# Two-stage attention and gated feed-forward kernel on one core: normalisation first in a step, an earlier first load, the decays of all heads later

## The chip, the cores and the metric

The kernel runs on one core of a Trainium2 chip. The metric is the device time of one execution in microseconds (us), lower being better. Differences of less than about 0.2% are not told from no change here.

## The reference

```python
# attention, B, H, S, D = 8, 8, 576, 64
scores = scale * np.matmul(q, k.transpose(0, 1, 3, 2))
log_f = np.log(np.clip(f, 0.0001, 1.0))
cum = np.cumsum(log_f, axis=-1)
decay = cum[:, :, :, None] - cum[:, :, None, :]
scores = np.where(causal, -1000000000.0, scores + decay)
scores = scores - np.max(scores, axis=-1, keepdims=True)
attn = np.exp(scores)
attn = attn / (np.sum(attn, axis=-1, keepdims=True) + 1e-09)
x = np.matmul(attn, v)                 # transposed and reshaped to 4608 x 512
# feed-forward, w_in 512 x 2048, w_out 2048 x 512
h = x @ w_in
sp = np.maximum(h, 0.0) + np.log1p(np.exp(-np.abs(h)))
out = (h * erf(sp)) @ w_out
```

`f` holds one gate for each head and position. Its clipped logarithm, summed along the sequence, is the decay that is added to the scores.

## The kernel before

The kernel has two stages. The first is the attention, which writes its output transposed to `xt_d` in HBM. The second is the feed-forward part (class `Moe`), which reads `xt_d` in chunks of 256 tokens. On TensorE (PE), VectorE (DVE), ScalarE (ACT) and GpSimd (POOL) the instructions stand in the order in which the code states them (`manual_schedule` with `ORDERED`, L20 and L230), and each engine works through its own list in that order. Only the DMA queue of SyncE (SP) is ordered by the scheduler.

**The step.** Heads are taken in 32 pairs, and each pair in two halves of its query blocks, so there are 64 units `t`, even and odd ones with other blocks (`BLOCKS`, `PARTS`, L34 to L42). The loop at L476 is a software pipeline. In step `t` it works on six units at once:

- `scores(t)` (L349): PE multiplies queries and keys of unit `t` into two PSUM tiles `s`, one for each head of the pair (`ps_s`, two buffers), and adds the causal mask (L363).
- `reduce(t, j)` (L373): DVE adds the decay `c` to the scores of head `j`, writes them to `pr` and takes the row extreme into `st`. With that the PSUM tile `s` of head `j` is free for `scores(t + 1)`.
- `exps(t - 1, j)` (L387): ACT applies Exp to `pr` in place and sums the rows into `st`.
- `normalize(t - 2)` (L394): DVE adds 1e-9 to the sums (L396) and takes reciprocals (L397). POOL then multiplies each row block of `pr` by its reciprocal (L401): four instructions for an even unit, six for an odd one.
- `transposes(t - 3, a)` (L404): PE transposes 128 x 128 blocks of `pr` into PSUM banks `t` (`ps_t`, three buffers): 12 blocks in three banks for an even unit, 13 in four for an odd one. `evacuate` copies a bank to `pt`: banks 0 and 1 by ACT (L422), banks 2 and 3 by DVE (L420, L418). Bank 3 takes the buffer of bank 0 again.
- `values(t - 4)` (L426): PE multiplies `pt` and the values into `o` (one PSUM buffer). `store(t - 5)` (L443): DVE copies `o` to `xo` (L449, L452, L453), and SP sends it to `xt_d`.

In an even step the transposes are thus those of an odd unit, and the other way round. One piece of weight conversion (`convert`, L277) stands near the end of each step from the fourth on: in turn ACT (L285), DVE (L289), DVE (L294 and L296), DVE with POOL (L299, L302, L303).

Before, DVE's list in a step reads: `store(t - 5)`, `reduce(t, 0)`, `reduce(t, 1)`, its evacuations of unit `t - 3`, `normalize(t - 2)`, `convert`.

**The start.** The pair 0 decays come from two rows of `f` that are broadcast to all partitions (`fd`): clip (L320, DVE), Ln (L321, ACT), running sum (L325, DVE), times -8 (L326, DVE). The same chain over all heads (`fr` to `cum`) goes to `cum_d` in HBM, and `load(p)` for later pairs broadcasts rows of `cum_d` into `c` (L340). Before, all of this stands ahead of the first step.

**The end of the attention.** For `t` from 64 to 67 each step also runs one `moe.step()` (L201): `up(j)` (PE, 24 matmuls, L126), `softplus(j)` (ACT, L132), and later `erf` and the gate. Softplus and Erf need other tables on ACT than Exp, so a table load stands before the first of them. Before, `moe.step()` stands last in the step. `load_x` and `split_x` (L100, L106) bring in a chunk of `xt_d` and split it in two parts on ACT (L111) and POOL (L112).

Of the kernel before, what the change touches and what calls it, by code (L numbers as in the profile page):

```python
# [11 lines left out]
F32 = mybir.dt.float32  # L12
# [9 lines left out]
P = 128  # L22
B, H, S, D = 8, 8, 576, 64
# [202 lines left out]
def attention_moe(ctx, tc, q2, k2, vp, f, w_in, w_out, out):  # L226
    nc = tc.nc
# [17 lines left out]
    cum_d = dram.tile([B * H, S], F32, name="cum_d")  # L245
# [10 lines left out]
    def wide4(nm):  # L256
        return cv.tile([P, 1024], F32, name=nm, tag="wide")

    moe = Moe(tc, xt_d, out, xp, wide4)
# [6 lines left out]
    def load_weight(u):  # L266

        a, i = divmod(u, 4)
        if i < 2:
            src = w_in[2 * i * P:2 * (i + 1) * P, a * 512:(a + 1) * 512].rearrange("(k p) n -> p k n", p=P)  # L270
        else:
            r = (2 * a + i - 2) * P
            src = w_out[r:r + P].rearrange("p (k n) -> p k n", k=2)
        raws[u] = raw = wide4(f"wraw{u}").bitcast(I32)
        nc.sync.dma_start(out=raw.rearrange("p (a n) -> p a n", a=2), in_=src)
# [35 lines left out]
    with ExitStack() as ph:  # L311
        early = ExitStack()
        wk = ph.enter_context(tc.tile_pool(name="wk", bufs=2))
# [5 lines left out]
        def log_clipped(x):  # L319
            nc.vector.tensor_scalar(out=x, in0=x, scalar1=1e-4, scalar2=1.0, op0=ALU.max, op1=ALU.min)  # L320
            nc.scalar.activation(out=x, in_=x, func=AF.Ln)  # L321

        def decay(out, x):

            nc.vector.tensor_tensor_scan(out=out, data0=x, data1=x, initial=0.0, op0=ALU.add, op1=ALU.bypass)  # L325
            nc.vector.tensor_scalar(out=out, in0=out, scalar1=-8.0, scalar2=None, op0=ALU.mult)  # L326
# [3 lines left out]
        def load(p):  # L330

            q = io.tile([P, PAD + S], F32, name=f"q{p}", tag="q")
            k = io.tile([P, S], F32, name=f"k{p}", tag="k")
            nc.sync.dma_start(out=q, in_=q2[p // NP, p % NP])
            nc.sync.dma_start(out=k, in_=k2[p // NP, p % NP])
            c = io.tile([P, 2, S], F32, name=f"c{p}", tag="c")
            if p:
                for j in range(2):
                    n = 2 * p + j
                    nc.sync.dma_start(out=c[:, j], in_=cum_d[n:n + 1].rearrange("a s -> (a s)").partition_broadcast(P))  # L340
            pairs[p] = [q, k, c]

        def load_values(p):

            v = wk.tile([P, 9, P], F32, name=f"v{p}", tag="v")
            nc.sync.dma_start(out=v, in_=vp[p // NP, p % NP].rearrange("p (c d) -> p c d", c=9))
            vals[p] = v
# [21 lines left out]
        def row(t, i, j):  # L369

            return probs[t][:, TOFF[i] + j * END[i]:TOFF[i] + (j + 1) * END[i]]

        def reduce(t, j):  # L373
            p, half = divmod(t, 2)
            c, s, st = pairs[p][2], raw_scores[t][j], stats[t]
            for m, i in enumerate(BLOCKS[half]):
                to, score, decay_ = (x.rearrange("p (k n) -> p k n", n=64) for x in (
                    row(t, i, j), s[:, SCOL[i]:SCOL[i] + END[i]], c[:, j, :END[i]]))
                nc.vector.tensor_tensor_reduce(  # L379
                    out=to[:, ::-1] if j else to, in0=score, in1=decay_, scale=-0.125, scalar=BIG,  # L380
                    op0=ALU.add, op1=ALU.min, accum_out=st[:, 0, j, m:m + 1])
            if j:
                del raw_scores[t]
                if half:
                    del pairs[p]

        def exps(t, j):  # L387
            st = stats[t]
            for m, i in enumerate(BLOCKS[t % 2]):
                seg = row(t, i, j)  # L390
                nc.scalar.activation(out=seg, in_=seg, func=AF.Exp, bias=st[:, 0, j, m:m + 1], scale=-1.0,  # L391
                                     accum_out=st[:, 1, j, m:m + 1])

        def normalize(t):  # L394
            st = stats.pop(t)
            nc.vector.tensor_scalar(out=st[:, 1], in0=st[:, 1], scalar1=1e-9, scalar2=None, op0=ALU.add)  # L396
            nc.vector.reciprocal(out=st[:, 2], in_=st[:, 1])  # L397
            for m, i in enumerate(BLOCKS[t % 2]):
                for j in range(2):
                    seg = row(t, i, j)  # L400
                    nc.gpsimd.tensor_scalar(out=seg, in0=seg, scalar1=st[:, 2, j, m:m + 1], scalar2=1.0,  # L401
                                            op0=ALU.mult, op1=ALU.mult)
# [12 lines left out]
        def evacuate(t, a):  # L415
            b, pt = banks.pop((t, a)), pts[t]
            if a == 3:
                nc.vector.tensor_copy(out=pt[:, 1536:], in_=b[:, 64:128])  # L418
            elif a == 2:
                nc.vector.tensor_copy(out=pt[:, 1024:1536], in_=b)  # L420
            else:
                nc.scalar.copy(out=pt[:, 512 * a:512 * a + 512], in_=b)  # L422
            if a == len(BANKS[t % 2]) - 1:
                del probs[t]
# [18 lines left out]
        def store(t):  # L443
            p, half = divmod(t, 2)
            o = held.pop(t)
            if half == 0:
                held["x"] = xo = wk.tile([P, S], F32, name=f"xo{p}", tag="xo")
                blocks = xo[:, 64:].rearrange("p (a q) -> p a q", a=4)
                nc.vector.tensor_copy(out=blocks[:, ::3], in_=o[:, :256].rearrange("p (a q) -> p a q", a=2))  # L449
            else:  # L450
                xo = held.pop("x")
                nc.vector.tensor_copy(out=xo[:, 192:448], in_=o[:, :256])  # L452
                nc.vector.tensor_copy(out=xo[:, :64], in_=o[:, 256:320])  # L453
                b, pp = divmod(p, NP)
                nc.sync.dma_start(out=xt_d[pp * P:(pp + 1) * P, b * S:(b + 1) * S], in_=xo)
                del vals[p]

        NH = B * H

        fd = [wk.tile([P, S], F32, name=f"fd{j}", tag=f"pt{j}") for j in range(2)]  # L460
        for j in range(2):
            nc.sync.dma_start(out=fd[j], in_=f[0, j].partition_broadcast(P))
        fr = wk.tile([B * H, S], F32, name="fr", tag="xo")
        nc.sync.dma_start(out=fr, in_=f.rearrange("b h s -> (b h) s"))
        load(0)
        for j in range(2):
            log_clipped(fd[j])
            decay(pairs[0][2][:, j], fd[j])
        log_clipped(fr)
        cum = wk.tile([B * H, S], F32, name="cum", tag="xo")  # L470
        decay(cum, fr)
        nc.sync.dma_start(out=cum_d, in_=cum)
        load(1)
        todo = pieces[1]
        load_weight(0)
        for t in range(NH + 5):  # L476
            there = [0 <= t - n < NH for n in range(6)]
            p, half = divmod(t, 2)
            if half == 0 and t + 4 < NH:
                load(p + 2)  # L480
            if half == 0 and there[2]:
                load_values(p - 1)
            if there[5]:
                store(t - 5)
            if there[0]:
                scores(t)
            if there[1]:
                exps(t - 1, 0)
            if there[0]:
                reduce(t, 0)  # L490
            if there[3]:
                for a in range(3):
                    transposes(t - 3, a)
                evacuate(t - 3, 0)
            if there[3] and len(BANKS[(t - 3) % 2]) == 4:
                transposes(t - 3, 3)
            if there[4]:
                values(t - 4)
            if there[1]:
                exps(t - 1, 1)  # L500
            if there[0]:
                reduce(t, 1)
            if there[3]:
                for a in range(1, len(BANKS[(t - 3) % 2])):
                    evacuate(t - 3, a)
            if there[2]:
                normalize(t - 2)
            if t >= 4 and todo:
                convert(*todo.pop(0))
            if t == NH - 2:  # L510
                moe.load_x(0)
                moe.split_x(0)
            if t == NH - 1:
                early.close()
                moe.ep = moe_pools.enter_context(tc.tile_pool(name="ep", bufs=2, side="right"))
                moe.ps_ha = moe_pools.enter_context(tc.tile_pool(name="ps_ha", bufs=4, space=PSUM, side="right"))
            if NH <= t < NH + 4:
                moe.step()
        assert not todo and not pts and not held and not vals

    w2 = ctx.enter_context(tc.tile_pool(name="w2", bufs=1))
# [44 lines left out]
```

## Time and profile before

| What | us |
|---|---|
| median of 3 runs | 1184.77 (1184.61 to 1186.2) |
| the profiled execution's own time | 1185.39 |
| its span in the profile | 1183.6 |
| PE busy | 1152.4 (97%) |
| DVE busy | 563.4 (48%) |
| ACT busy | 598.9 (51%) |
| POOL busy | 474.1 (40%) |

The own time of the profiled execution is 1.8 us more than the span from the first to the last instruction. PEld is the loading of PE's weights, which overlaps its matmuls. In a timeline row stand start, busy time, engine, line, operation, tiles, shape, count, and in brackets the idle time before the row with what ended it. A row can hold several instructions that follow each other. In a table of windows the engines' busy times in each stretch are followed by PEclk, the granted TensorE clock as a share of full speed. The attention fills the span to about 348 us, the feed-forward part the rest.

### The profile page before, as it was taken

Reading aid. Unit: us, or ns where it says so; the run is one execution under the profiler, and the core shown is the slowest. Engines: PE = TensorE matmul, PEld = TensorE weight load, DVE = VectorE, ACT = ScalarE, POOL = GpSimd, SP = SyncE. Lnnn points to the kernel's source line nnn. Section 1 sums busy time; section 2 is a strip of 40 time slices with the busy share of each in tenths; the row PEclk is TensorE's granted clock in tenths of the full one; section 3 lists DMA queues with packets and bytes.
Section 4 is the critical chain, followed back from the end, with each engine's and each line's share of the span. In section 5 each row is a group of like instructions: output and inputs, shape, how many; then the busy total and the mean of one; then the engine's idle time right before and its main releaser. Section 6 shows DMA issues by size and latency. Waiting matters only on the chain.

```text
span 1183.6 us, 22838 instructions
## 1 busy us (share of the span) xinstructions
PE 1152.4 (97%) x8992; PEld 1010.0 (85%) x8992; DVE 563.4 (48%) x1473; ACT 598.9 (51%) x1231; POOL 474.1 (40%) x531
## 2 busy tenths in 40 slices
PE   5999999999999999999999999999999999999998
PEld 3777777777779999999999999998999999998987
DVE  4888888888874665665322322321231231231221
ACT  3777777777775676565423422432432342242432
POOL 1565666555673444444432432232232232232221
PEclk9999999999999999999999999999999999999999
DMA  7566767667641222421221221210110110100000
GB/s 249 187 229 230 240 215 244 213 220 239 208 145 56 79 100 75 139 73 54 89 72 54 77 85 54 71 37 1 37 36 1 36 35 2 37 15 23 18 19 18
DMA packets 56618, 118.68 MB, mean 100 GB/s; under 512 B 4672, under 2 KB 19008, under 8 KB 56512
## 3 DMA queue, kind: packets, MB, share of 16 engines
q1 hardware_dynamic: 56512, 117.23, 30.2%
q8 instruction: 71, 1.16, 0.4%
q14 instruction: 35, 0.29, 0.1%
HBM read 93.47 MB, written 23.74 MB: 99 GB/s over the span
## 4 chain that ended last, share of the span: by engine, by line
PE 82%; DVE 9%; POOL 7%; issue 1%; ACT 1%; DMA 0%; POOLq 0%; ACTq 0%
PE ph L126 35%; PE y L165 11%; PE y L163 11%; PE y L164 11%; POOL pr L401 7%; DVE pr L379 6%; PE s L358 5%; PE o L440 4%; PE t L413 3%; DVE pt L420 2%; PE s L363 1%; DVE st L397 1%; DMA fd<-in_f_dram 0%; DVE c L325 0%; DVE st L396 0%
## 5 line engine op out<-in xcount | busy, mean ns | idle before, releaser
L126 PE MATMUL ph<-xh,w 128*128 128x256 f32 x2304 | 435.8, 282 | 0.0
L126 PEld LDWEIGHTS ph<-xh,w 128*128 128x128 f32 x2304 | 367.0, 191 | 5.9
L144 POOL TENSOR_TENSOR gl<-e,gh 128x512 fp32r<-128x512 f32 x144 | 186.8, 1297 | 354.0 <-DVE gh L143 348.7
L126 PE MATMUL ph<-xl,w 128*128 128x256 f32 x1152 | 325.0, 282 | 0.0
L132 ACT ACTIVATE e<-ph 128x512 f32<-128x512 f32 x144 | 86.2, 598 | 448.3 <-PE ph L126 447.9
L401 POOL TENSOR_SCALAR pr<-pr,st 128x576 f32<-128x576 f32 (+4 forms) x320 | 179.9, 580 | 160.6 <-DVE st L397 132.7
L165 PE MATMUL y<-w,gl 128*128 128x512 f32 x576 | 228.2, 396 | 0.0
L163 PE MATMUL y<-w,gh 128*128 128x512 f32 x576 | 228.1, 396 | 0.0
L164 PE MATMUL y<-w,gh 128*128 128x512 f32 x576 | 227.2, 394 | 0.0
L126 PEld LDWEIGHTS ph<-xl,w 128*128 128x128 f32 x1152 | 219.3, 190 | 5.7
L391 ACT ACTIVATE pr<-pr,st 128x576 f32<-128x576 f32 (+3 forms) x320 | 176.5, 555 | 8.4 <-DVE st L379 8.4
L143 DVE CAST gh<-e 128x512 fp32r<-128x512 f32 x144 | 86.6, 601 | 174.6 <-PE y L164 163.0
L379 DVE CUSTOM_DVE_ANT_0 pr<-s,c 128x576 f32<-128x576 f32 (+3 forms) x320 | 136.5, 485 | 54.4 <-PE s L363 46.3
L141 DVE TENSOR_TENSOR e<-e,ph 128x512 f32<-128x512 f32 x144 | 97.9, 680 | 103.1 <-ACT e L135 101.7
L165 PEld LDWEIGHTS y<-w,gl 128*128 128x128 f32 x576 | 108.7, 189 | 25.9
L358 PE MATMUL s<-k,q 64*128 64x320 f32 (+4 forms) x768 | 114.8, 424 | 13.4 <-DMA k<-in_k_dram 8.3
L164 PEld LDWEIGHTS y<-w,gh 128*128 128x128 f32 x576 | 108.8, 189 | 20.7
L413 PE MATMUL t<-ident,pr 128*128 128x128 f32 x800 | 112.5, 281 | 14.0 <-POOL pr L401 12.9
L112 POOL TENSOR_TENSOR xl<-xr,xh 128x1024 fp32r<-128x1024 f32 x27 | 65.8, 2439 | 149.3 <-ACT xh L111 149.3
L163 PEld LDWEIGHTS y<-w,gh 128*128 128x128 f32 x576 | 108.8, 189 | 19.7
L422 ACT COPY pt<-t 128x512 f32<-128x512 f32 x128 | 73.6, 577 | 82.0 <-PE t L413 82.0
L358 PEld LDWEIGHTS s<-k,q 64*128 64x128 f32 x768 | 75.4, 194 | 43.4 <-issue 18.7
(50 smaller groups left out, 1009.3 us busy)
## 6 DMA issues: line engine op xcount, KB each, us to landing
v<-in_vp_dram SPq DMA_DIRECT2D x32, 576.0 KB, 6.1
c<-cum_d SPq DMA_DIRECT2D x62, 288.0 KB, 4.8
xr<-xt_d SPq DMA_DIRECT2D x27, 512.0 KB, 4.1
q<-in_q_dram SPq DMA_DIRECT2D x32, 320.0 KB, 2.9
k<-in_k_dram SPq DMA_DIRECT2D x32, 288.0 KB, 3.4
xt_d<-xo SPq DMA_DIRECT2D x32, 288.0 KB, 5.7
wraw<-in_w_in_dram SPq DMA_DIRECT2D x16, 512.0 KB, 5.7
wraw<-in_w_out_dram SPq DMA_DIRECT2D x16, 512.0 KB, 5.5
```

What stands on the lines that cost most here:

```text
L126: nc.tensor.matmul(out=ps[:, e], lhsT=w[:, kd, fs], rhs=x[:, kd], start=kd == 0 and n == 0, stop=kd == KD - 1 and n == 2)
L141: nc.vector.tensor_mul(e_, e_, h_)
L143: nc.vector.tensor_copy(out=gh, in_=e_)
L144: nc.gpsimd.tensor_tensor(out=gl, in0=e_, in1=gh.bitcast(F32), op=ALU.subtract)
L163: nc.tensor.matmul(out=y[tb], lhsT=gh[:, cs], rhs=wh[:, e], start=first, stop=False)
L164: nc.tensor.matmul(out=y[tb], lhsT=gh[:, cs], rhs=wl[:, e], start=False, stop=False)
L165: nc.tensor.matmul(out=y[tb], lhsT=gl[:, cs], rhs=wh[:, e], start=False, stop=last)
L358: nc.tensor.matmul(out=s[j][:, at:at + k1 - k0], lhsT=q[h, PAD + START[i]:PAD + END[i]], rhs=k[h, k0:k1], start=i > 0, stop=k1 < END[i])
L379: nc.vector.tensor_tensor_reduce(out=to[:, ::-1] if j else to, in0=score, in1=decay_, scale=-0.125, scalar=BIG, op0=ALU.add, op1=ALU.min, ...
L391: nc.scalar.activation(out=seg, in_=seg, func=AF.Exp, bias=st[:, 0, j, m:m + 1], scale=-1.0, accum_out=st[:, 1, j, m:m + 1])
L401: nc.gpsimd.tensor_scalar(out=seg, in0=seg, scalar1=st[:, 2, j, m:m + 1], scalar2=1.0, op0=ALU.mult, op1=ALU.mult)
L413: nc.tensor.transpose(out=b[:, n * P:(n + 1) * P], in_=probs[t][:, at:at + P], identity=ident)
```

## The change

Four statements move; no instruction of the computation is added or dropped.

1. `normalize(t - 2)` goes from the end of a step to its beginning, ahead of `store(t - 5)`.
2. `moe.step()` in steps 64 to 67 goes from the end of the step to its beginning, ahead of `normalize`.
3. The loads of pair 0 are issued behind the first `fd` row and ahead of the second and of `fr`.
4. The decays of all heads, with the `cum_d` store, `load(1)`, `load(2)` and the first weight load, are stated between `reduce(0, 0)` and `reduce(0, 1)`. The loop's `load(p + 2)` starts at `t` = 2 instead of 0.

```diff
         fd = [wk.tile([P, S], F32, name=f"fd{j}", tag=f"pt{j}") for j in range(2)]
-        for j in range(2):
-            nc.sync.dma_start(out=fd[j], in_=f[0, j].partition_broadcast(P))
+        nc.sync.dma_start(out=fd[0], in_=f[0, 0].partition_broadcast(P))
+        load(0)
+        nc.sync.dma_start(out=fd[1], in_=f[0, 1].partition_broadcast(P))
         fr = wk.tile([B * H, S], F32, name="fr", tag="xo")
         nc.sync.dma_start(out=fr, in_=f.rearrange("b h s -> (b h) s"))
-        load(0)
...
-        log_clipped(fr)
-        cum = wk.tile([B * H, S], F32, name="cum", tag="xo")
-        decay(cum, fr)
-        nc.sync.dma_start(out=cum_d, in_=cum)
-        load(1)
         todo = pieces[1]
-        load_weight(0)
+
+        def all_decays():
+            log_clipped(fr)
+            cum = wk.tile([B * H, S], F32, name="cum", tag="xo")
+            decay(cum, fr)
+            nc.sync.dma_start(out=cum_d, in_=cum)
+            load(1)
+            load(2)
+            load_weight(0)
...
-            if half == 0 and t + 4 < NH:
+            if half == 0 and 0 < t < NH - 4:
                 load(p + 2)
             if half == 0 and there[2]:
                 load_values(p - 1)
+            if NH <= t < NH + 4:
+                moe.step()
+            if there[2]:
+                normalize(t - 2)
             if there[5]:
                 store(t - 5)
...
             if there[0]:
                 reduce(t, 0)
+                if t == 0:
+                    all_decays()
...
-            if there[2]:
-                normalize(t - 2)
...
-            if NH <= t < NH + 4:
-                moe.step()
```

The first place is DVE in the middle of the attention, from the end of an odd step into an even one. The `st` tiles tell the units apart. Before, the unit with `st_3038` is normalised here: it is the odd unit two before the odd step that ends.

```order
L420 COPY pt_3202<-t_2_3213 128x512
L396 TENSOR_SCALAR st_3038<-st_3038 128x6
L397 RECIPROCAL st_3038<-st_3038 128x6
L289 SCALAR_TENSOR_TENSOR wtop_3177<-wtop_3177,wraw_3096 128x512
L452 COPY xo_3179<-o_3219 128x256
L453 COPY xo_3179<-o_3219 128x64
L379 ISA pr_3276,st_3277<-s_0_3264,c_2944 128x576
```

In the changed kernel the same stretch of DVE's list reads as follows; `st_3129` is the even unit two before the even step that begins.

```order
L420 COPY pt_3210<-t_2_3221 128x512
L289 SCALAR_TENSOR_TENSOR wtop_3177<-wtop_3177,wraw_3096 128x512
L396 TENSOR_SCALAR st_3129<-st_3129 128x4
L397 RECIPROCAL st_3129<-st_3129 128x4
L452 COPY xo_3187<-o_3227 128x256
L453 COPY xo_3187<-o_3227 128x64
L379 ISA pr_3282,st_3283<-s_0_3270,c_2944 128x576
```

The pair of instructions stays at nearly the same place, but it now serves the next unit: each unit is normalised a good half step to a whole step sooner.

The second place is DVE at the start. Before, the decays of all heads (`fr`, `cum`) stand ahead of the first reduction of the scores:

```order
L326 TENSOR_SCALAR c_126<-c_126 128x576
L320 TENSOR_SCALAR fr<-fr 64x576
L325 SCALAR_TENSOR_TENSOR cum<-fr 64x576
L326 TENSOR_SCALAR cum<-cum 64x576
L379 ISA pr_169,st_170<-s_0_157,c_126 128x576
L379 ISA st_170 128x1
L379 ISA pr_169,st_170<-s_0_157,c_126 128x192
L379 ISA st_170 128x1
L379 ISA pr_169,st_170<-s_1_158,c_126 128x9x64
```

In the changed kernel they stand behind the reduction of the first head (`s_0`) and ahead of that of the second (`s_1`):

```order
L326 TENSOR_SCALAR c_123<-c_123 128x576
L379 ISA pr_147,st_148<-s_0_135,c_123 128x576
L379 ISA st_148 128x1
L379 ISA pr_147,st_148<-s_0_135,c_123 128x192
L379 ISA st_148 128x1
L320 TENSOR_SCALAR fr<-fr 64x576
L325 SCALAR_TENSOR_TENSOR cum<-fr 64x576
L326 TENSOR_SCALAR cum<-cum 64x576
L379 ISA pr_147,st_148<-s_1_136,c_123 128x9x64
```

What stands ahead of the reduction of `s_1` is the same work in another order.

The third place is ACT at the end of the attention, in step 64. Before, the last Exp rows (`st_4902`) stand ahead of the first softplus (`e_5051`), and one table load is between them:

```order
L391 ACTIVATE pr_4901,st_4902<-pr_4901,st_4902 128x448
L391 ACTIVATE pr_4901,st_4902<-pr_4901,st_4902 128x320
L391 ACTIVATE pr_4901,st_4902<-pr_4901,st_4902 128x64
L422 COPY pt_4978<-t_0_4979 128x512
L391 ACTIVATE pr_4901,st_4902<-pr_4901,st_4902 128x448
L391 ACTIVATE pr_4901,st_4902<-pr_4901,st_4902 128x320
L391 ACTIVATE pr_4901,st_4902<-pr_4901,st_4902 128x64
L422 COPY pt_4978<-t_1_4984 128x512
L285 ACTIVATE wtop_5024<-wraw_4960 128x512
L132 ACT_TABLE_LOAD
L132 ACTIVATE e_5051<-ph_5026 128x512
```

In the changed kernel the first softplus (`e_4997`) stands ahead of the last Exp rows (`st_4910`):

```order
L422 COPY pt_4916<-t_1_4922 128x512
L132 ACT_TABLE_LOAD
L132 ACTIVATE e_4997<-ph_4972 128x512
L391 ACT_TABLE_LOAD
L391 ACTIVATE pr_4909,st_4910<-pr_4909,st_4910 128x448
L391 ACTIVATE pr_4909,st_4910<-pr_4909,st_4910 128x320
L391 ACTIVATE pr_4909,st_4910<-pr_4909,st_4910 128x64
L422 COPY pt_5011<-t_0_5012 128x512
```

A third load stands further on, ahead of the second softplus. ACT now goes from the Exp table to softplus, back, and to softplus again: two table loads more. On PE, `up(0)` to `up(3)` stand each ahead of the transposes and values of their step instead of behind them.

## The prediction

> **What bounds the kernel now.** I read the page first, then PE's waits, the windows, and the timeline of two steps in the middle of the attention. These are the page's engine line, rows of PE's waits over the whole span, the feed-forward window, and PE's one wait between 40 and 320 us (total, times, longest).
>
> ```profile
> PE 1152.4 (97%) x8992; PEld 1010.0 (85%) x8992; DVE 563.4 (48%) x1473; ACT 598.9 (51%) x1231; POOL 474.1 (40%) x531
> ...
> PE t L413 <- POOL pr L401: 12.9, 34, 1.4
> PE s L358 <- DMA k<-in_k_dram: 8.3, 1, 8.3
> ...
> 600.00:800.00 200.00, 200.00 (x1269) 180.77 (x1268) 54.94 (x89) 71.30 (x97) 64.53 (x43) 1.00 0.20 64
> ...
> PE t L413 <- POOL pr L401: 9.9, 28, 0.4
> ```
>
> PE bounds both stages. In the feed-forward part it is busy 200 of 200 us, and the change leaves the order there as it was, so nothing can come from it. In the attention the one thing that PE waits for, once running, is POOL: the transposes wait for normalised rows. The timeline shows where; PE, the reciprocals and POOL over two steps and a bit, then the mean of POOL's 448- and 320-wide multiplications:
>
> ```profile
> 200.33 1.57 PE L358 MATMUL s<-k,q 64*128 64x320 f32 x12
> 200.47 0.19 DVE L397 RECIPROCAL st<-st 128x6 f32<-128x6 f32 x1
> 200.86 3.25 POOL L401 TENSOR_SCALAR pr<-pr,st 128x448 f32<-128x448 f32 x6 [3.02 <-DVE st L397]
> 202.06 1.16 PE L413 MATMUL t<-ident,pr 128*128 128x128 f32 x7
> 203.58 0.91 PE L413 MATMUL t<-ident,pr 128*128 128x128 f32 x6 [0.36 <-POOL pr L401]
> 204.42 1.54 PE L440 MATMUL o<-pt,v 128*64 128x128 f32 x28
> 205.89 1.73 PE L358 MATMUL s<-k,q 64*128 64x448 f32 x12
> 207.85 1.51 PE L413 MATMUL t<-ident,pr 128*128 128x128 f32 x12
> 209.28 1.66 PE L440 MATMUL o<-pt,v 128*64 128x128 f32 x32
> 210.88 1.57 PE L358 MATMUL s<-k,q 64*128 64x320 f32 x12
> 212.61 1.01 PE L413 MATMUL t<-ident,pr 128*128 128x128 f32 x7
> 213.98 0.91 PE L413 MATMUL t<-ident,pr 128*128 128x128 f32 x6 [0.36 <-POOL pr L401]
> 214.81 1.54 PE L440 MATMUL o<-pt,v 128*64 128x128 f32 x28
> ...
> L401 POOL TENSOR_SCALAR pr<-pr,st 128x448 f32<-128x448 f32 x38 | 29.7, 793 | 61.4 <-DVE st L397 58.1 <-ACT pr L391 3.3
> L401 POOL TENSOR_SCALAR pr<-pr,st 128x320 f32<-128x320 f32 x38 | 19.7, 528 | 0.0
> ```
>
> An even step runs from 200.33 to 205.89, an odd one from there to 210.88. The even step transposes an odd unit, whose reciprocals were ready only at 200.66, inside the same step. POOL begins at 200.86; two 448-wide rows and two 320-wide ones end at 200.86 + 2 x 0.793 + 2 x 0.528 = 203.50, and PE's eighth transpose starts at 203.58. So the wait is POOL's. In the odd step twelve transposes take 209.28 - 207.85 = 1.43 us with no wait.
>
> PE's idle time understates the loss, because the modelled end of a matmul covers part of the gap. I count start to start. The 13 transposes of an even step take 204.42 - 202.06 = 2.36 us, or 214.81 - 212.61 = 2.20, by turns. At the odd step's rate they would take 13/12 x 1.43 = 1.55. So an even step loses 0.81 or 0.65 us.
>
> **Part 1, normalisation first.** Two DVE instructions for each unit move, and four or six POOL instructions follow them. The odd unit's reciprocals now stand at the head of the odd step instead of at its end. They can run from 205.10, when the Exp sums are there (below), so POOL's 3.25 us end near 209, against the next even step's transposes at 212.61. The even unit's move from the end of the even step to its head in the same way; its four POOL rows are fewer and its transposes come in the odd step, at 207.85, so POOL has over 2 us to spare there too. The POOL wait goes in every even step from `t` = 4 to 62: 30 steps.
>
> What is late next? The rows around the boundary, of ACT and DVE:
>
> ```profile
> 202.99 0.59 ACT L422 COPY pt<-t 128x512 f32<-128x512 f32 x1 [1.16 <-PE t L413]
> 203.47 0.67 ACT L391 ACTIVATE pr<-pr,st 128x448 f32<-128x448 f32 x1
> 204.91 0.19 ACT L391 ACTIVATION_READ_ACCUMULATOR pr<-pr,st 128x1 f32 x1
> 206.01 0.42 DVE L449 COPY xo<-o 128x256 f32<-128x256 f32 x1 [0.43 <-PE o L440]
> 208.02 0.62 DVE L379 CUSTOM_DVE_ANT_0 pr<-s,c 128x448 f32<-128x448 f32 x1 [1.58 <-PE s L363]
> 210.22 0.69 DVE L420 COPY pt<-t 128x512 f32<-128x512 f32 x1
> ```
>
> The moved reciprocal adds a wait to DVE: at the head of the odd step it needs the sums of Exp, complete at 204.91 + 0.19 = 205.10. Behind it are queued the copy of `o` (0.42) and the reduction, which waits for PE's scores until 208.02 anyway. With about 0.4 for the two instructions and 0.45 for the copy DVE is done near 206.0, so some 2 us cover it in a step as it is, and 1.2 us in one that is 0.8 shorter. The reduction ends at 210.22, 0.66 ahead of the scores that need its buffer (210.88); the odd step doesn't get shorter, so that slack stays. The thirteenth transpose needs bank 0, which ACT empties in 0.59. ACT starts 0.93 after the first transpose (202.99 - 202.06), with 0.15 of waiting in it (seven transposes in 1.16 against 1.01 at 212.61), so without that the bank is free 0.78 + 0.59 = 1.37 after their start, plus the signal, against 1.43 for PE to get there. That is close, so I allow 1.60 instead of 1.55 for the 13.
>
> Gain: 30 x ((2.36 + 2.20)/2 - 1.60) = 30 x 0.68 = 20.4 us. Its bounds are 30 x 0.73 = 22 (no new wait at all) and, if a new wait takes half, 10.
>
> **Parts 3 and 4, the start.** DVE's second `fd` row, the last reduction of unit 0, the read-back of the decays, scores of PE, and the first reduction that needs those decays:
>
> ```profile
> 7.44 0.45 DVE L320 TENSOR_SCALAR fd<-fd 128x576 f32<-128x576 f32 x1
> ...
> 15.27 0.07 DVE L379 DVE_READ_ACCUMULATOR2_ANT st<- 128x1 f32 x1
> ...
> 17.30 1.76 SPq L340 DMA_DIRECT2D c<-cum_d  x4
> 20.42 4.04 PE L358 MATMUL s<-k,q 64*128 64x320 f32 x12 [1.06 <-issue]
> ...
> 24.82 0.76 DVE L379 CUSTOM_DVE_ANT_0 pr<-s,c 128x576 f32<-128x576 f32 x1 [3.41 <-PE s L363]
> ```
>
> PE's first matmul waits 8.3 us for `k`. `k` is now the third of the five first loads instead of the fifth, so PE will start sooner, by 1.5 to 2 us as I estimate from two loads of five less. But that isn't the path. The second unit's scores need both `s` tiles, and the second is free when DVE's reduction ends at 15.34. DVE runs through the two `fd` chains, the `fr` chain and the reductions one behind the other, and the change only reorders these. One thing moves against it: the second `fd` row, now behind `q` and `k` on SP's queue, lands nearer to the 8.3 us at which all five loads were there, so its clip starts at about 7.75 instead of 7.44. I put down +0.3, with the bounds 0 and 0.9 (8.3 - 7.44). The `cum_d` store now stands behind the first head's reduction, about 1.1 us (0.76 for its 576-wide part at 24.82, and a 192-wide one), so the read-back at 17.30 begins near 18.4; its four issues and landing of some 5 us fit ahead of 24.82, with a microsecond to spare. If that cover is gone, the cost is what is missing, up to 1 us. Here PE still runs slowly: the 12 score matmuls at 20.42 take 4.04 us with one wait in them, those at 200.33 take 1.57. A step more or less of that would be worth some 2 us either way; I forecast no change.
>
> **Part 2, the feed-forward steps first.** Rows of the transition: PE's waits, ACT's tables, and the granted clock (in windows of 1 us, PEclk is third from the end):
>
> ```profile
> 348.74 0.55 PE L413 MATMUL t<-ident,pr 128*128 128x128 f32 x3 [1.39 <-POOL pr L401]
> 354.42 0.38 PE L126 MATMUL ph<-xh,w 128*128 128x256 f32 x1
> 357.39 1.47 PE L413 MATMUL t<-ident,pr 128*128 128x128 f32 x12
> 357.59 0.60 ACT L132 ACTIVATE e<-ph 128x512 f32<-128x512 f32 x1 [3.19 <-PE ph L126]
> ...
> 366.07 1.28 ACT L135 ACT_TABLE_LOAD   x1
> ...
> 367.37 1.16 ACT L135 ACTIVATE e<-e 128x512 f32<-128x512 f32 x2
> 370.48 1.66 PE L440 MATMUL o<-pt,v 128*64 128x128 f32 x32
> ...
> 350.00:351.00 1.00, 0.65 (x5) 0.47 (x4) 0.00 (x0) 1.00 (x3) 1.00 (x3) 0.83 1.12 429
> 353.00:354.00 1.00, 1.00 (x14) 1.00 (x12) 0.00 (x0) 0.98 (x2) 0.87 (x2) 0.50 1.02 397
> ```
>
> Step 64 starts at 348.74 - 1.39 = 347.35. Values of unit 63 start at 370.48 and take 1.6, and `up(3)` takes 357.39 - 354.42 = 2.97, so the four steps end near 375.05: 27.7 us. The work alone is 4 x 2.97, transposes of 1.55 + 1.43 + 1.55 and values of 2 x 1.47 + 2 x 1.6: 22.5. So 5.2 us are lost, part of it because the granted clock fell to half from about 350.7 to 354.0, behind the wait of 1.39 and two short ones.
>
> Now `up(0)` covers the POOL wait. But ACT's queue holds softplus, which waits for `up(0)`, then a table load and the last Exp rows ahead of bank 0's copy: 0.2 (357.39 to 357.59) + 0.60 + 1.28 + 1.63 (203.47 to 205.10) + 0.59 = 4.3 us from the end of `up(0)`. PE has 12 transposes, 1.43 us, until it needs that bank: a new wait of 2.9 us. A second, which I estimate at 0.5, comes in step 66, where softplus, held up by Erf and its table loads, stands ahead of the same copy. Loss 3.4, so 1.8 us less than before, if the clock holds. Here a wait of 1.39 was enough to halve it for 3.3 us, which costs 1.65; with 2.9 I take that to happen again: 1.8 - 1.65, a gain of 0.1. Bounds: a gain of 1.8, a loss of 2 (one further wait of the same kind).
>
> The Trainium skill ("TensorE: Matmul & The Clock Gate", Why this matters for your kernels) advises no idle gap of PE over about 3 us; by that the clock would hold, and the sum would be 1.65 us lower. This trace disagrees, with its drop behind 1.39 us. The Trainium skill ("ScalarE: Activation LUTs", What ACT_TABLE_LOAD costs) adds a drain of about 1.38 us to each switch, which would lengthen the new wait by that much. The trace shows none: the load at 366.07 takes 1.28, and Erf starts at 367.37.
>
> **The sum.** -20.4 + 0.3 - 0.1 = -20.2. From the profiled execution's 1185.39 that gives 1165.2; the median is 0.6 lower, so on its scale 1164.6. That is 1.7% faster; about 0.2% (2.4 us) is what can be told from no change.
>
> **Rivals.**
> - *The gain is half given back* (0.15): with shorter steps DVE's evacuations and weight conversion reach past PE's scores, the reduction ends late, and PE waits for a PSUM tile. For: DVE has only 0.66 us ahead of 210.88. Against: odd steps keep their length, and DVE sits idle 1.58 us ahead of 208.02. It would give 1164.6 + 10 = about 1175.
> - *No change* (0.04): the wait put down to POOL is really for an ACT-emptied bank, so PE waits on. Against: POOL's rows end where PE starts, to 0.1 us. Only the transition and the start would act: 1184.9.
> - *Slower* (0.03): DVE's new wait for the Exp sums, at the head of the odd step, holds up the copy of `o` and the reduction behind it. From 1.2 us of lateness of ACT on, PE waits; at 2.2 us late each pair loses 1.0 against 0.68 won, which is 30 x 0.32 = 10 us: 1195. Against: ACT's sums are there at 205.10, before DVE needs them.
> - *Forecast* (0.78).
>
> With 0.78 on the forecast the range is its own bounds, with some of the first rival: below, no new wait (-1.6) and a held clock (-1.65), 1161; above, the start's and the transition's upper ends (+0.6, +2.1) and a third of the first rival's loss (+3.5), 1171. Faster by over 0.2%: 0.78 + 0.15 = 0.93, less 0.02 for a rival that takes more than half. Within 0.2%: 0.05. Slower: 0.04.
>
> **What would show it.** Right: PE's wait for POOL between 40 and 320 us is gone, the 13 transposes take 1.55 to 1.65 start to start, even steps 4.75 to 4.85 and odd ones 4.98; one PE wait of some 3 us near step 64 for an ACT copy, and PE's first matmul near 6.3 with the second unit's scores no sooner than before. Wrong: waits of PE's scores for the reductions in the middle, a reduction of DVE behind a late Exp sum, or transposes that still take 2.2 us.

## The result and the profile after

| What | before, us | after, us |
|---|---|---|
| median of 4 runs each, on one chip | 1185.39 (1184.61 to 1186.2) | 1166.18 (1166.04 to 1166.36) |
| span of the profiled execution | 1183.6 | 1164.3 |
| scores of unit 6 start | 43.32 | 44.13 |
| scores of unit 63 start | 342.29 | 324.92 |
| `up(0)` to `up(3)` with their transposes and values end | 375.05 | 355.6 |

The ratio is 0.9838, with a 95% interval from 0.9821 to 0.9855. The kernel is 19.2 us faster, and the prediction's 1164.6 is 1.6 us too low.

The three positions split the 19.3 us of the span. The start, with the first improved step in it, costs 0.81 (44.13 - 43.32). The middle, units 6 to 63, gains 18.18 (298.97 against 280.79). The rest, 1.93, is gained in the four steps 64 to 67: 27.7 us before, and 355.6 - 329.9 = 25.7 after. Behind them both kernels take the same time.

The page's engine line of the changed kernel, two rows of PE's waits over the whole span (total, times, longest), and PE's only wait between 40 and 315 us:

```profile
PE 1144.3 (98%) x8992; PEld 1010.2 (87%) x8992; DVE 547.6 (47%) x1473; ACT 601.7 (52%) x1233; POOL 459.8 (39%) x531
...
PE t L413 <- DVE pt L420: 1.7, 2, 0.9
...
PE t L413 <- POOL pr L401: 0.9, 2, 0.6
...
PE t L413 <- POOL pr L401: 0.2, 1, 0.2
```

The 28 waits for POOL in the middle have become one of 0.2. Nothing came in their place there. What is new are the two waits for a DVE copy, both in the transition from the attention to the feed-forward part. DVE and POOL are less busy than before by 15.8 and 14.3 us, though they do the same work; the last section comes back to it.

The timeline of the changed kernel over two steps of the middle, reciprocals, POOL and PE:

```profile
196.57 0.19 DVE L397 RECIPROCAL st<-st 128x6 f32<-128x6 f32 x1
196.95 2.86 POOL L401 TENSOR_SCALAR pr<-pr,st 128x448 f32<-128x448 f32 x6 [0.47 <-ACT pt L422]
203.36 1.73 PE L413 MATMUL t<-ident,pr 128*128 128x128 f32 x13
204.76 0.14 PEld L413 LDWEIGHTS t<-ident,pr 128*128 128x128 f32 x1 [0.16 <-POOL pr L401]
205.02 1.54 PE L440 MATMUL o<-pt,v 128*64 128x128 f32 x28
```

An odd unit's reciprocals are done at 196.76, POOL's six rows at 196.95 + 2.86 = 199.81, and its transposes start at 203.36: 3.5 us to spare, where POOL was up to 0.8 late before. The 13 transposes take 205.02 - 203.36 = 1.66 instead of 2.36 and 2.20. The 0.16 at 204.76 is put down to POOL, but POOL had long been done; it is taken up below (e4).

### The profile page after: what moved, and what is told of

It is laid out like the page before. It is cut to its first block, busy times and chain, and to the rows that moved or that the text cites. A ratio compares the mean times of both kernels' runs of the same rounds, so it can differ in the third digit from the quotient of the medians.

```text
span 1164.3 us, 22871 instructions
## 1 busy us (share of the span) xinstructions
PE 1144.3 (98%) x8992; PEld 1010.2 (87%) x8992; DVE 547.6 (47%) x1473; ACT 601.7 (52%) x1233; POOL 459.8 (39%) x531
## 4 chain that ended last, share of the span: by engine, by line
PE 97%; DVE 1%; DMA 1%; ACT 1%; POOL 0%; issue 0%; SPq 0%; POOLq 0%
PE ph L126 35%; PE y L165 12%; PE y L163 12%; PE y L164 11%; PE s L358 9%; PE o L440 8%; PE t L413 8%; PE s L363 2%; DMA fd<-in_f_dram 1%; POOL pr L401 0%; DVE pr L379 0%; DVE pt L420 0%; DVE c L325 0%; DVE cum L325 0%; ACT L135 0%
## 5 line engine op out<-in xcount | busy, mean ns | idle before, releaser
L401 POOL TENSOR_SCALAR pr<-pr,st 128x576 f32<-128x576 f32 (+4 forms) x320 | 165.2, 538 | 120.5 <-DVE st L397 90.9
L112 POOL TENSOR_TENSOR xl<-xr,xh 128x1024 fp32r<-128x1024 f32 x27 | 65.7, 2432 | 157.0 <-ACT xh L111 154.2
L413 PE MATMUL t<-ident,pr 128*128 128x128 f32 x800 | 104.3, 276 | 2.6 <-DVE pt L420 1.7
```

The costliest lines, as they stand in the source:

```text
L413: nc.tensor.transpose(out=b[:, n * P:(n + 1) * P], in_=probs[t][:, at:at + P], identity=ident)
```

## The experiments

Eight kernels were run, each in five rounds together with the kernel before, whose median was 1185.19 us in the first four and 1185.18 in the last four. They split the change into its parts: part 1 (normalisation first), part 2 (`moe.step()` first), parts 3 (loads) and 4 (decays of all heads), which make the new start.

| Kernel | parts | median, us | ratio to before, 95% interval |
|---|---|---|---|
| e1_norm_only | 1 | 1163.25 | 0.9814 (0.98 to 0.9827) |
| e2_start_only | 3, 4 | 1185.72 | 1.0005 (0.9996 to 1.0014) |
| e3_norm_moe | 1, 2 | 1164.77 | 0.9826 (0.9813 to 0.984) |
| e4_bank3_late | 1, 2, bank 3 later | 1165.34 | 0.9832 (0.9819 to 0.9846) |
| e5_moe_only | 2 | 1184.56 | 0.9992 (0.9983 to 1.0001) |
| e6_fd_first | 1, 2, 4 | 1166.14 | 0.9837 (0.9824 to 0.9851) |
| e8_load_sooner | 1, 2, 3 | 1165.52 | 0.9833 (0.9819 to 0.9846) |
| e7_norm_mid | a smaller dose of 1 | 1172.34 | 0.9887 (0.9872 to 0.9903) |
| the changed kernel | 1 to 4 | 1166.18 | 0.9838 (0.9821 to 0.9855) |

The differences among e1, e3, e6, e8 and the changed kernel are 0.04 to 2.9 us, mostly less than 0.2%, and the intervals of their ratios overlap. What carries them are the four times of each kernel, whose ranges follow each other: e1 1162.57 to 1164.0, e3 1164.41 to 1165.0, e8 1165.31 to 1165.89, e6 1165.83 to 1166.4 and the changed kernel 1166.04 to 1166.36. Their order is thus fairly sure, except between e8 and e6, which just touch, and between e6 and the changed kernel; their sizes are good to about half a microsecond.

### e1: part 1 alone

```diff
+            if there[2]:
+                normalize(t - 2)
             if there[5]:
                 store(t - 5)
...
-            if there[2]:
-                normalize(t - 2)
```

> Part 1 alone: normalisation first in a step, everything else as before. Theory (the gain is the POOL wait in the 30 even steps, 0.63 us each): even steps 4.87 us instead of 5.56 and 5.41 by turns, 18.8 us in all, and in step 64 the POOL wait of 1.39 shrinks below 0.7, so about 1165 us. Rival (part 2, the feed-forward steps first, carries a share of the gain of 2 us or more): 1168 or above.

It is the fastest of all: 1163.25, which is 21.9 us less than before, 2.9 less than the changed kernel, and below the 1165 or so that was expected. Units 6 to 63 take 280.79, to the hundredth what the changed kernel takes, so the whole gain of the middle is part 1's. It also does more than the prediction gave it. The four steps 64 to 67 fall from 27.7 to 24.4 us by it alone, because the wait for POOL of 1.39 in step 64 shrinks with all the others, and because the granted clock, which fell to 0.50 in step 64 before, stays at 1.00 here. The clock is about half of it: in e2, which has the old wait and a full clock, the four steps take 26.1 us. PE's rows of e1 in steps 64 to 67:

```profile
329.10 1.09 PE L413 MATMUL t<-ident,pr 128*128 128x128 f32 x6 [0.34 <-POOL pr L401]
...
342.89 0.30 PE L413 MATMUL t<-ident,pr 128*128 128x128 f32 x1 [0.89 <-ACT pt L422]
...
347.65 1.66 PE L440 MATMUL o<-pt,v 128*64 128x128 f32 x32
```

Only 0.34 for POOL in step 64 and 0.89 for a copy in step 66 are left. So parts 2 to 4 together cost 2.9 us, and the next runs divide that.

### e3: parts 1 and 2

```diff
# against e1
+            if NH <= t < NH + 4:
+                moe.step()
             if there[2]:
                 normalize(t - 2)
...
-            if NH <= t < NH + 4:
-                moe.step()
```

> Parts 1 and 2 without the new start, so the changed kernel with the old start. Theory (the new start costs 1.3 to 2.0 us): 1164.2 to 1164.9 us, faster than the changed kernel. Rival (the later times at the start were chance, or made up by the pipeline): 1166.2 as the changed kernel.

With 1164.77, as the theory said, it is 1.5 us slower than e1 and 1.4 faster than the changed kernel. So part 2, given part 1, is a loss of 1.5, and the new start one of 1.4. The transition of the changed kernel shows part 2's loss, which e3's rows repeat:

```profile
333.08 0.60 ACT L132 ACTIVATE e<-ph 128x512 f32<-128x512 f32 x1 [1.91 <-PE ph L126]
333.69 1.28 ACT L391 ACT_TABLE_LOAD   x1
334.39 0.69 DVE L420 COPY pt<-t 128x512 f32<-128x512 f32 x1 [2.21 <-PE t L413]
335.23 0.30 PE L413 MATMUL t<-ident,pr 128*128 128x128 f32 x1 [0.88 <-DVE pt L420]
336.54 0.56 ACT L422 COPY pt<-t 128x512 f32<-128x512 f32 x1
338.88 0.19 DVE L397 RECIPROCAL st<-st 128x6 f32<-128x6 f32 x1
342.62 2.40 POOL L112 TENSOR_TENSOR xl<-xr,xh 128x1024 fp32r<-128x1024 f32 x1 [7.19 <-ACT xh L111]
344.99 3.14 POOL L401 TENSOR_SCALAR pr<-pr,st 128x448 f32<-128x448 f32 x6
347.60 0.77 PE L413 MATMUL t<-ident,pr 128*128 128x128 f32 x5 [0.64 <-POOL pr L401]
349.24 0.30 PE L413 MATMUL t<-ident,pr 128*128 128x128 f32 x1 [0.87 <-DVE pt L420]
354.01 1.66 PE L440 MATMUL o<-pt,v 128*64 128x128 f32 x32
```

ACT does what the prediction said: softplus, a table load, three Exp rows, and bank 0's copy only at 336.54. But the thirteenth transpose of unit 61 runs at 335.23, ahead of that copy, so it can't have waited for it. It waited for DVE's copy of bank 2, which ends at 334.39 + 0.69 = 335.08. The order of the two programs says why, in PE's list with the engines that the thirteenth transposes of units 61 and 63 wait for (before, then the changed kernel; e3 and e5 have the latter):

```
1699 L413 MATMUL t61_3_4995<-ident_63,pr61_4748 128x128 [waits Activation_49,Pool_49]
1755 L413 MATMUL t63_3_5153<-ident_63,pr63_4901 128x128 [waits Activation_49,Pool_49]

1716 L413 MATMUL t61_3_5028<-ident_63,pr61_4756 128x128 [waits DVE_49,Pool_49]
1772 L413 MATMUL t63_3_5188<-ident_63,pr63_4909 128x128 [waits DVE_49,Pool_49]
```

In the 30 odd units before these bank 3 still waits for ACT. In the two where `moe.step()` stands ahead, the pool gives bank 3 another buffer, that of bank 2. In step 64 PE then waits 0.88 for it, where e1 waits 0.34 for POOL. The 0.87 in step 66 is no new cost: e1 waits 0.89 at the same transpose for ACT (its row at 342.89), and so does the kernel before.

What is new in step 66 is the wait of 0.64 for POOL at 347.60. The reciprocals of unit 63 are done at 338.88 + 0.19 = 339.07, but POOL begins with its rows only at 344.99. Ahead of them in POOL's list stands the split of the next chunk (L112). It is a piece of `moe.step()` and moved ahead with it, and it waits until 342.62 for ACT's part of the split. In e3 the 13 transposes take 2.58 and 3.61 in the two steps, in e1 2.35 and 2.59. So step 64 accounts for 0.23 and step 66 for 1.02 of the 1.5 us.

### e5: part 2 alone

```diff
# against before
+            if NH <= t < NH + 4:
+                moe.step()
             if there[5]:
                 store(t - 5)
...
-            if NH <= t < NH + 4:
-                moe.step()
```

> Only the feed-forward steps are stated first (part 2 alone, with normalisation and start as before). Theory: part 2 is a matter of what it covers. Without part 1 the transposes of unit 61 and 63 wait longest for POOL (0.36 and 1.39 us before), and up(0) now stands in front of step 64's, so the four steps 64 to 67, 27.7 us before, should come to 25.5 to 26.5, with the granted clock at 1.00 throughout: 1183 to 1184, 1 to 2 us less than before. Rival: what part 2 cost beside part 1 (1164.77 against 1163.25) is its own price wherever it stands: 1186.7, 1.5 us more than before. The steady steps stay at 5.56 and 4.98 in both.

The four steps take 25.84 us (27.7 before), as the theory said, with a granted clock of 1.00 in the window from 348 to 375. Most of that is the clock: e2, with the old order of these steps and a full clock, takes 26.1. The 13 transposes show two effects that nearly cancel. In step 64 they take 2.58 in e5 and 4.03 in e2, so covering the wait of 1.39 gains 1.45. In step 66 they take 3.67 in e5 and 2.59 in e2, a loss of 1.08. That loss is the same with part 1 (1.02 in e3) and without it, so it is a price of part 2 wherever it stands. The gain depends on what there is to cover, and with part 1 there is almost nothing. In the median only 0.6 us of the expected 1 to 2 arrived (1184.56 against 1185.18, and the interval includes no change), so this total is not told from zero. Units 6 to 63 took 299.49 in its profile against 298.97, which took 0.5 of it; the 13 transposes were 2.38 instead of 2.36 there, as they are in e2 (299.47 for these units), and why stays open.

### e2: the new start alone

The changed kernel with `normalize(t - 2)` and `moe.step()` back at their old places.

> Parts 3 and 4 alone: pair 0 loaded sooner, decays of all heads between the first two reductions; normalisation and feed-forward steps where they were before. Theory (the first decay row lands 1 us later because q and k share the DMA engines with it, and DVE's chain of decays, which is the path, ends 1.3 us later): 1.3 to 2.0 us slower than before, about 1187 us, with the first reduction of the second score tile done near 16.7 us instead of 15.3. Rival (PE's earlier first matmul counts): 0.8 us faster than before.

With 1185.72 it is 0.5 us slower, less than expected, and not told from no change. In its profile the start does cost 1.36: scores of unit 6 begin at 44.68 instead of 43.32. Units 6 to 63 take 0.5 more, and what brings 1.6 back are the four steps 64 to 67, 26.1 us instead of 27.7. PE's wait and values in step 64 and the granted clock (third from the end) behind the wait, in e2, then the values of the same step in the kernel before:

```profile
350.60 0.55 PE L413 MATMUL t<-ident,pr 128*128 128x128 f32 x3 [1.39 <-POOL pr L401]
353.24 1.54 PE L440 MATMUL o<-pt,v 128*64 128x128 f32 x28
352.00:353.00 1.00, 0.64 (x7) 0.55 (x6) 0.00 (x0) 1.00 (x4) 1.00 (x4) 1.00 1.11 428
...
351.93 2.57 PE L440 MATMUL o<-pt,v 128*64 128x128 f32 x28
```

The wait is 1.39, the same as before, and the clock stays at 1.00, where it fell to 0.50 before; the 28 matmuls behind it take 1.54 instead of 2.57. So the length of this wait alone doesn't decide whether the clock falls. The unprofiled runs agree that the start costs something where the clock holds: the two runs of the kernel before with a mean granted clock of 1.00 took 1184.45 and 1184.77 us, the six of e2 with 1.00 took 1185.45 to 1185.81.

### e6 and e8: what the new start costs

```diff
# e6, against the changed kernel: its loads in the old order
-        nc.sync.dma_start(out=fd[0], in_=f[0, 0].partition_broadcast(P))
-        load(0)
-        nc.sync.dma_start(out=fd[1], in_=f[0, 1].partition_broadcast(P))
+        for j in range(2):
+            nc.sync.dma_start(out=fd[j], in_=f[0, j].partition_broadcast(P))
...
+        load(0)
# e8, against e3: its loads in the new order, all else as in e3
-        for j in range(2):
-            nc.sync.dma_start(out=fd[j], in_=f[0, j].partition_broadcast(P))
+        nc.sync.dma_start(out=fd[0], in_=f[0, 0].partition_broadcast(P))
+        load(0)
+        nc.sync.dma_start(out=fd[1], in_=f[0, 1].partition_broadcast(P))
...
-        load(0)
```

> The changed kernel with the loads in the order of before (both fd rows, fr, then q and k of pair 0) and the decays of all heads where the change put them. Theory: the 1.4 us that the new start costs come from the fd rows that land about 1 us later while q and k are under way, which every DVE instruction up to reduce(0, 1) inherits; so the fd0 clip starts near 4.5 again, reduce(0, 1) ends near 15.3, and the time is 1164.8, like parts 1 and 2 with the old start. Rival: the place of the decays costs it (reduce(0, 1) comes behind them, and cum_d is written later): 1166.2, like the changed kernel.

> Parts 1 and 2 with the loads in the order of the change (fd0, q and k of pair 0, fd1, fr), but the decays of all heads ahead of the first step as before. Theory of the late fd rows: the fd0 clip starts near 5.4, reduce(0, 1) ends near 16.7, and the time is 1166.2. Rival, the place of the decays: 1164.8. If both parts cost something, the two kernels lie between and their losses add up to 1.4.

e6 gives 1166.14, 1.4 more than e3: its theory fell, and the place of the decays alone costs as much as the whole new start. e8 gives 1165.52, 0.75 more than e3: the new load order costs something too. The two losses add up to 2.1, yet together, in the changed kernel, they cost 1.4. The rows say how. DVE's first clip in the kernel before; then DVE's waits and PE's scores of units 0 and 2 in the changed kernel:

```profile
4.46 0.46 DVE L320 TENSOR_SCALAR fd<-fd 128x576 f32<-128x576 f32 x1 [2.39 <-DMA fd<-in_f_dram]
...
5.43 0.46 DVE L320 TENSOR_SCALAR fd<-fd 128x576 f32<-128x576 f32 x1 [3.35 <-DMA fd<-in_f_dram]
8.78 0.46 DVE L320 TENSOR_SCALAR fd<-fd 128x576 f32<-128x576 f32 x1 [0.28 <-DMA fd<-in_f_dram]
16.62 0.07 DVE L379 DVE_READ_ACCUMULATOR2_ANT st<- 128x1 f32 x1
...
7.48 2.93 PE L358 MATMUL s<-k,q 64*128 64x320 f32 x12 [7.48 <-DMA k<-in_k_dram]
21.76 4.04 PE L358 MATMUL s<-k,q 64*128 64x320 f32 x12 [1.06 <-issue]
```

In e6, with the loads in the old order:

```profile
4.55 0.46 DVE L320 TENSOR_SCALAR fd<-fd 128x576 f32<-128x576 f32 x1 [2.47 <-DMA fd<-in_f_dram]
11.54 0.76 DVE L379 CUSTOM_DVE_ANT_0 pr<-s,c 128x576 f32<-128x576 f32 x1 [0.96 <-PE s L363]
16.41 0.07 DVE L379 DVE_READ_ACCUMULATOR2_ANT st<- 128x1 f32 x1
```

And in e8, with the decays at the old place:

```profile
4.93 0.46 DVE L320 TENSOR_SCALAR fd<-fd 128x576 f32<-128x576 f32 x1 [2.85 <-DMA fd<-in_f_dram]
15.87 0.07 DVE L379 DVE_READ_ACCUMULATOR2_ANT st<- 128x1 f32 x1
```

Before, DVE finished the last reduction of unit 0 at 15.34. In the changed kernel that is 16.69, in e6 16.48, in e8 15.94, and the scores of unit 2 move with it (20.42 before, then 21.76, 21.56 and 21.02). In e6 the first reduction stands directly behind the `fd` chains and waits 0.96 for PE's first scores, a time in which the decays of all heads ran before. In e8 the first `fd` row lands later, with `q` and `k` on their way at the same time. In the changed kernel the `fd` rows are later still: DVE waits 0.96 more for the first and 0.28 for the second, and by then PE's scores are there. So the one loss hides a part of the other. The profiles are single executions, and the first clip varies by half a microsecond among kernels whose start is the same (4.21 in e3, 4.72 in e7), so the sizes are taken from the medians.

### e4: the thirteenth transpose

```diff
# against e3
-            if there[3] and len(BANKS[(t - 3) % 2]) == 4:
-                transposes(t - 3, 3)
             if there[4]:
                 values(t - 4)
+            if there[3] and len(BANKS[(t - 3) % 2]) == 4:
+                transposes(t - 3, 3)
```

> Parts 1 and 2 with the old start, and the thirteenth transpose (bank 3 of an odd unit) stated behind the values of the step on PE instead of ahead of them. Theory (what is left over 1.55 us in the 13 transposes, 0.11 us a step, is the wait for bank 0, which ACT empties): even steps 4.76 instead of 4.87, 30 x 0.11 = 3.3 us less than the same kernel without this, about 1161 us. Rival (the 0.11 is another cost of the thirteenth transpose, or DVE's copy of bank 3, now later, holds up the reductions): no change, or slower by up to 0.2 us a step.

PE's list of e4 in an even step:

```profile
202.40 1.48 PE L413 MATMUL t<-ident,pr 128*128 128x128 f32 x12
203.81 1.54 PE L440 MATMUL o<-pt,v 128*64 128x128 f32 x28
205.29 0.33 PE L413 MATMUL t<-ident,pr 128*128 128x128 f32 x1
205.55 1.72 PE L358 MATMUL s<-k,q 64*128 64x448 f32 x11
```

Twelve transposes take 1.41 and the thirteenth, now with 1.5 us of other work between, still takes 205.55 - 205.29 = 0.26 instead of the 1.43/12 = 0.12 of one in a row. The steps stay at 4.87, and the time is no better. So the 0.06 to 0.11 us above the prediction's figures are not the wait for bank 0; what makes a single transpose dearer wasn't found.

### e7: a smaller dose of part 1

```diff
# against before
+            if there[2]:
+                normalize(t - 2)
             if there[3]:
                 for a in range(1, len(BANKS[(t - 3) % 2])):
                     evacuate(t - 3, a)
...
-            if there[2]:
-                normalize(t - 2)
```

> A smaller dose of part 1: normalisation is stated ahead of DVE's late evacuations of the step instead of behind them, at most some 0.7 to 0.9 us sooner than before, and not half a step; everything else as before. Theory (the even step waits because POOL's rows are 0.65 to 0.81 us late, and nothing else): most of the gain is there already, the 13 transposes take 1.65 to 1.8, and the time is 1163 to 1167. Rival (the gain needs POOL's work away from DVE's conversion, or DVE can't run the reciprocals sooner because the Exp sums are not there): the 13 transposes still take over 2 us and the time is 1177 or more.

1172.34 (1170.06 to 1173.83): 12.8 us faster, 59% of what e1 gains. The theory said nearly all, and the rival 1177 or more, so neither range holds it. The 13 transposes take 1.97 and 1.81 by turns. Rows of e7, the reciprocals and PE of two even steps, and two groups of POOL rows with a conversion of DVE:

```profile
189.04 2.90 POOL L401 TENSOR_SCALAR pr<-pr,st 128x576 f32<-128x576 f32 x4 [1.18 <-ACT pr L391]
190.10 1.14 DVE L296 SCALAR_TENSOR_TENSOR wraw<-wraw 128x512 int32<-128x512 int32 x1
199.69 2.27 POOL L401 TENSOR_SCALAR pr<-pr,st 128x576 f32<-128x576 f32 x4 [0.43 <-ACT pt L422]
204.33 0.19 DVE L397 RECIPROCAL st<-st 128x6 f32<-128x6 f32 x1
206.51 1.88 PE L413 MATMUL t<-ident,pr 128*128 128x128 f32 x13
208.32 1.54 PE L440 MATMUL o<-pt,v 128*64 128x128 f32 x28
214.67 0.19 DVE L397 RECIPROCAL st<-st 128x6 f32<-128x6 f32 x1
216.50 0.95 PE L413 MATMUL t<-ident,pr 128*128 128x128 f32 x7
...
L401 POOL TENSOR_SCALAR pr<-pr,st 128x448 f32<-128x448 f32 x64 | 53.5, 849 | 83.7 <-DVE st L397 74.7 <-ACT pt L422 3.2 <-PE o L440 2.9
```

The reciprocals are done 206.51 - 204.52 = 1.99 and 216.50 - 214.86 = 1.64 ahead of the transposes, against 1.40 before (202.06 - 200.66). The dose is 0.59 and 0.24, not the 0.7 to 0.9 of the expectation, and POOL's 448-wide row has become slower, 849 ns against 791. So the size of the expectation was wrong, and the loss does fall with the lateness: where POOL is a part of the way less late, PE waits a part less.

## Why the prediction was right, and where it was not

**Part 1, -20.4: right in mechanism, nearly right in size.** Over the 30 even steps the 13 transposes took 68.9 us before and 50.0 after: 18.9 won. The figure of 1.60 for them was 1.66 in all but the first steps. The reason given for the 0.05 above 1.55, PE arriving at bank 0 close to ACT's copy, fell with e4. The two things that were looked for as late next, DVE's wait for the Exp sums and the reductions, don't show: PE has no wait for a reduction between 40 and 315 us, and odd steps kept 4.98. That refutes the first and the third rival. The second, that the wait was not POOL's, is refuted by e1.

What the prediction left out is that part 1 acts in the transition too. It charged the 1.39 of step 64 to part 2's account, and e1 shows that part 1 alone takes 3.3 us out of these four steps, 1.6 of it by the clock that doesn't fall.

**Parts 3 and 4, +0.3 with an upper bound of 0.9: too small; 1.4 by e3 against the changed kernel.** Two steps failed. It took the first `fd` row as unmoved, being still first on SP's queue, and moved only the second; but its clip started at 5.43 instead of 4.46, with `q` and `k` right behind it. (That the transfers share the DMA engines is the likely reason, but no run shows it.) And it said that DVE only does "the same work in another order"; but the decays of all heads filled the time until PE's first scores were there, and e6 shows 0.96 us of waiting once they don't. That the start of PE is not the path was right: PE began at 7.48, 0.85 sooner (1.5 to 2 were predicted), and the scores of unit 2 came 1.34 later.

**Part 2, -0.1: the sum of two effects that were both wrong.** The new wait of 2.9 us for ACT's copy of bank 0 didn't come. ACT was as late as predicted: the copy ended at 337.10, 4.2 us behind the end of `up(0)` at 332.88 (4.3 predicted). But bank 3 didn't take the buffer of bank 0 there: the pool handed it that of bank 2, and PE waited 0.88 for DVE. The step that failed is the assumption that a buffer's turn stays as it is when statements move; the waits in PE's list show the change ahead of any run. In step 66 the prediction looked for 0.5 more at ACT's copy; a wait of 0.89 was there already, and what came on top was the 0.64 for POOL, behind a split that the prediction didn't consider. The renewed fall of the clock (1.65) didn't come either, and e2 shows that even 1.39 doesn't always bring it. (The price of one fall was right: 1.65 predicted, 1.6 by e2.) Against before's transition the changed kernel gains 2.0, close to the 1.8 that the prediction gave for a clock that holds. That is luck: none of it is part 2's, which costs 1.5 given part 1.

**The sum.** By the medians part 1 gives -21.9, part 2 +1.5 and the start +1.4: 1166.2, as measured (the three are the steps from before to e1, e3 and the changed kernel, so they must add up). The forecast of 1164.6 came out of a gain that was 1.5 too low, a part 2 that was 1.6 too kind, and a start 1.1 too kind: 1.2 in all. The other 0.4 is the kernel before, whose median was 1184.77 in the runs shown and 1185.19 beside the experiments. So the mechanism of the large term was right, and that the total came within 1.6 us is in part luck, as errors of 1.1 to 1.6 us went both ways.

## What to carry to other kernels

Where an engine is late by less than a microsecond in every step, move what it waits for to the head of the step, and look for the same wait at the edges of the loop, where it can be larger. A statement that seems to sit idle in a prologue may fill a wait: ask, before moving it, what its engine will wait for at that place. When a rotating pool decides who waits for whom, read the engines that each instruction waits for from the compiled order of the changed kernel, and don't carry a buffer's turn over from before. A step that moves takes its pieces on all engines with it, so look at what they now stand ahead of on each. And keep of a change only the parts that pay: e1, one statement moved, beats both kernels.

## What the runs showed of the hardware

**DVE and POOL slow each other.** No instruction was added or removed on POOL or DVE, and both are busy for about 15 us less. POOL's 448-wide multiplication over its 64 rows, and DVE's L296 between 40 and 330 us (min, median, max), in the changed kernel:

```profile
L401 POOL TENSOR_SCALAR pr<-pr,st 128x448 f32<-128x448 f32 x64 | 40.3, 642 | 51.8 <-DVE st L397 28.5 <-ACT pr L391 11.3 <-ACT pt L422 6.6
...
L296 DVE SCALAR_TENSOR_TENSOR wraw<-wraw x15: 693/694/699, 49.2 to 325.1; 128x512 int32<-128x512 int32 x15
```

The same two in the kernel before:

```profile
L401 POOL TENSOR_SCALAR pr<-pr,st 128x448 f32<-128x448 f32 x64 | 50.0, 791 | 102.9 <-DVE st L397 99.5 <-ACT pr L391 3.3
...
L296 DVE SCALAR_TENSOR_TENSOR wraw<-wraw x14: 1124/1127/1127, 48.7 to 321.3; 128x512 int32<-128x512 int32 x14
```

In e7's rows above the overlap is seen at work: four POOL rows take 2.90 with L296 among them and 2.27 without, and L296 takes 1.14. In the changed kernel POOL's rows of an odd unit fall in part (1.58 of the 2.86 us from 196.95) where DVE waits for scores, and where L296 runs, at 206.65, POOL is idle. The Trainium skill ("SBUF — State Buffer", Who interferes with whom) says that a DVE instruction with two inputs in SBUF contends with a GpSimd instruction that reads SBUF; L296 reads two, and the trace agrees, with 1.127 against 0.694 us. It was no term of the sum, and since neither engine bounds the middle it moves the time only where POOL is late, as in e7.

**The granted clock** fell behind a wait of 1.39 us in the profile of before and not behind the same wait in e2's. The Trainium skill ("TensorE: Matmul & The Clock Gate", Why this matters for your kernels) advises against gaps over about 3 us; e2 agrees with it, the kernel before doesn't, and what decides between them is open. One candidate, which no run tests, is the whole stretch in which PE only waited and transposed: 4.6 us before (347.35 to 351.93) and 4.0 in e2 (349.21 to 353.24). At the start the profiles differ as well. From 16 to 28 us the granted clock was 0.50 in e1, e3, e4, e5 and e7 and 1.00 in the other five. The totals don't show it: the five runs of e5 with a mean clock of 0.993, like its profile with that fall, have a median of 1184.62, its four with 0.999 one of 1184.54.

**A small load ahead of large ones is not safe from them.** The first `fd` row was issued first in all kernels, and DVE waited 3.35 us for it in the changed kernel instead of 2.39 before, once `q` and `k` followed it directly. In the three profiles with that order its clip starts at 4.93 to 5.43, in the seven others at 4.21 to 4.72.
